# Six of 36 input loads issued as two transfers (rows 0 to 119 and rows 120 to 127) in a retention and token-mixing kernel

## The chip, the cores and the metric

The kernel runs on one core of a Trainium2 chip. The metric is the device time of one execution in microseconds (us), as the median of several runs. TensorE is called PE below, VectorE DVE, ScalarE ACT, GpSimd POOL; SyncE (SP) issues the transfers (DMAs) between HBM and on-chip memory.

## What is computed

Two stages. The first is a retention recurrence over the tokens of each of 4 batches and 8 heads, with 64 x 64 states:

```python
for t in range(S):                      # S = 768
    state = gamma * state + outer(k[t], v[t])
    y[t] = scale * q[t] @ state
```

The second stage takes x, the heads of y side by side (4 x 768 x 512), and mixes tokens:

```python
W_tok = scale * (x @ w_q) * (x @ w_k)   # einsum bsd,btd->bst
out = relu(W_tok @ x) @ w_out
```

q, k and v are float32 of shape 4 x 8 x 768 x 64 each, the output is float32 of shape 4 x 768 x 512.

## The kernel before

The 768 tokens of a batch are cut into three **pairs** of two chunks of 128 tokens, 12 pairs in all (0 to 11). Each pair needs a load of q, of k and of v, so there are 36 loads of 512 KB. A pair has a kind (`KINDS`): R, 2 or M. A load (function `load`) fills one slot of the tile `stage`, 128 partitions x 1024 floats. In q and k loads of every kind, and in v loads of kinds R and 2, one transfer brings the whole slot: partition g gets tokens 2g and 2g+1 of all eight heads, so 8 pieces of 512 bytes for each of 128 partitions. A v load of kind M (pairs 9, 10 and 11) takes four transfers of 128 KB. The first v load is split over two issuing engines, ACT and SP; SP issues every other transfer, in one queue.

Everything runs in an order written out by hand (`ORDER`): each word of it is a step, and each engine takes its own steps in that order. `Lk.4=11` is the load of k of pair 4 into slot 11. SP's order is v0, k0, q0, q1, k1, k2, q2, v1, q3, k3, v2, k4, v3, W (the two small weights), q4, q5, k5, v4, LO (w_out, in four pieces), v5, k6, q6, q7, v6, k7, v7, k9, q8, k8, q9, v8, v9, k11, q10, k10, v10, q11, v11, and then 15 stores of the output. The loads up to v7 go into fresh slots; from k9 on a load first waits until its slot has been read, and a store until its slot has been written.

A load is followed by casts to bf16: `ck` and `cq` make `ks` and `qs` of k and q (line 145 on ACT, 146 on DVE and POOL), `cv` makes `vs` of v with the decay factors `fv` (lines 380 and 399, mostly on POOL). On PE follow the transposes of k and q (lines 471 to 517), the scores `sc` (line 556), the state update `st` (line 590, from `ks` and `vs`), the two halves of y (`in` lines 629 to 650, `ia` lines 669 and 683), and the second stage: transposes of x (713, 719), `wqk` (746, 757), `zm` (783), `mx` (802), and the output projection `pj` (824), whose results go back into `stage` for the stores (line 216). `fill` (line 345) are matmuls on a tile of zeros that stand at fixed places of the order. DMA lines are 188 (whole loads), 183 (v of kind M), 198 and 205 (weights), 216 (stores).

Of the kernel before, what the change touches and what calls it, by code (L numbers as in the profile page):

```python
# [63 lines left out]
SLOTS = 27  # L64
U = 2
PAD = 224
BUFS = dict(
    ks=6, vs=6, qs=4, kT=3, qT=3, at0=2, at1=2, s=4, x=6, xT=3, m=7, z=2, relu=4,
)
# [5 lines left out]
def kernel(  # L75
# [21 lines left out]
    B, H, S, D = q.shape  # L97
# [14 lines left out]
    def pool(name, bufs, **kw):  # L112
        return ctx.enter_context(tc.tile_pool(name=name, bufs=bufs, **kw))


    pool("pad", 1).tile([128, PAD], FP32, name="pad")
    stage_pool = pool("stage", 1)
    const_pool = pool("const", 1)
    pools = {name: pool(name, bufs) for name, bufs in BUFS.items()}
    psum = pool("psum", 1, space=bass.MemoryType.PSUM)  # L120
# [27 lines left out]
    def rows(i):  # L148
        return slice(i * 64, i * 64 + 64)
# [6 lines left out]
    def tokens(p):  # L156
        b, cp = divmod(p, NP)
        return b, slice(cp * 2 * C, (cp + 1) * 2 * C)

    def load(name, p, slot, part=None, eng=None):  # L160
        eng = eng or nc.sync
        b, ts = tokens(p)
        src = {"k": k, "q": q, "v": v}[name][b, :, ts, :]
        st = stage[:, slot]
        pairs[p][name + "_st"] = st
        cs = range(2) if part is None else (part,)
        hs = slice(0, H) if part is None else slice(part, H, 2)
        if name == "q" and U == 8:
            f = slice(0, 2) if part is None else part
            eng.dma_start(  # L170
                out=st.rearrange("p (x f) -> p x f", x=2)[:, f],
                in_=src.rearrange("h (t u) d -> t h (u d)", u=U)[:, hs],
            )
        elif KINDS[p] == "N" and name != "q":
            for c in cs:
                eng.dma_start(
                    out=st[:, 512 * c : 512 * c + 512].rearrange("t (h d) -> t h d", d=D),
                    in_=src[:, C * c : C * c + C].rearrange("h t d -> t h d"),
                )
        elif KINDS[p] == "M" and name == "v":  # L180
            for c in cs:
                for j in range(2):
                    eng.dma_start(
                        out=st[rows(j), 512 * c : 512 * c + 512].rearrange("g (h d) -> g h d", d=D),
                        in_=src[:, C * c : C * c + C].rearrange("h (g j) d -> j g h d", j=2)[j],
                    )
        else:
            eng.dma_start(  # L188
                out=st.rearrange("g (h f) -> g h f", h=H)[:, hs],
                in_=src.rearrange("h (g j) d -> g h (j d)", j=2)[:, hs],  # L190
            )

    wstages = {}

# [15 lines left out]
    def store(p, c=None):  # L210
# [5 lines left out]
        nc.sync.dma_start(out=dst, in_=src, max_dma_last_dim=OBYTES)  # L216

    load(*FIRST, 0, nc.scalar)
    load(*FIRST, 1, nc.sync)


# [76 lines left out]
    if U > 2:  # L298
# [3 lines left out]
            out=ident_q.rearrange("p (c hp t) -> p c t hp", c=2, hp=HP),  # L302
            in_=identity.rearrange("p (c t hp) -> p c t hp", c=2, hp=HP),
# [16 lines left out]
    for cp in range(NP):  # L320
        nc.vector.tensor_copy(
            out=fy1.rearrange("p (cp x) c hp -> p cp x c hp", x=2)[:, cp].rearrange("p x c hp -> p c x hp"),
            in_=fy[:, 2 * cp : 2 * cp + 2].rearrange("p c (hp x) -> p c x hp", x=2),
# [521 lines left out]
    for token in ORDER:  # L845
        token, _, slot = token.partition("=")
        token, _, b = token.partition("@")
        token, _, e = token.partition(":")
        name, *args = token.split(".")
        if b:  # L850
            b = ["ab".index(i) if i in "ab" else int(i) for i in b]
        args = [int(i) for i in args]
        if name == "fill":
            fill(args[0], b[0])
        elif name == "W":
            W(e)
        elif name in ("Lk", "Lq", "Lv"):
            load(name[1], args[0], int(slot))
        elif name == "LW":
            load_w(int(slot))  # L860
        elif name == "LO":
            load_wo(args[0], int(slot))
        elif name == "S":
            store(*args)
        elif name == "eo":
            eo(e, b, *args, slot=int(slot))
        else:
            steps[name](e, b, *args)
# [30 lines left out]
```

## Time and profile before

| | |
|---|---|
| median of 3 runs | 101.84 us (101.64 to 101.92) |
| profiled execution | 101.69 us, of which 99.8 us from the first to the last instruction (the span) |
| PE busy | 89.9 us, 90% of the span |
| DVE, ACT, POOL busy | 74.2, 70.1, 51.8 us |
| moved by DMA | 26.73 MB in 47169 packets, mean 268 GB/s |
| read from HBM, written | 20.19 MB, 6.29 MB |
| granted PE clock | 1.0 throughout |

A row of the profile gives the line of the code, the engine, the operation and its tiles (out<-in). A name with a q behind an engine (SPq) is that engine's sequencer, here SP issuing a transfer. The time that a row of SPq shows is the time that the issue took on SP, not the time until the data lands.

### The profile page before, as it was taken

The page shows a single profiled execution, that of the slowest core. Times are in us where ns is not written, and L with a number is a line of the kernel's source. Part 1 is how long each engine was busy: PE and PEld are TensorE (multiplying, and loading weights), DVE is VectorE, ACT ScalarE, POOL GpSimd, SP SyncE. Part 2 cuts the span into 40 slices and gives each one's busy share as a digit, 9 for nine tenths or more (in the row PEclk, how much of TensorE's full clock was granted, in tenths as well). Part 3 has the DMA queues.
Part 4 walks back from the last instruction along what each step waited for, and adds up shares of the span by engine and source line. Part 5 has one row for each costly group of instructions (what it writes and reads, how often), then busy time and mean ns, then how long its engine had stood idle before and what let it go on. Part 6 is the DMA issues. An engine that isn't in the chain of part 4 may idle for free.

```text
span 99.8 us, 3840 instructions
## 1 busy us (share of the span) xinstructions
PE 89.9 (90%) x1642; PEld 59.9 (60%) x1642; DVE 74.2 (74%) x123; ACT 70.1 (70%) x124; POOL 51.8 (52%) x68
## 2 busy tenths in 40 slices
PE   5996999999599979989998997999999999999940
PEld 1335476587488656676786473676786775754310
DVE  6495789998677998897669887889869865360340
ACT  5245694599769799956588967899669785339720
POOL 6091318253892968958499999977892000000000
PEclk9999999999999999999999999999999999999999
DMA  0999999999999999999998999989933920591793
GB/s 19 301 346 348 346 347 344 323 275 267 277 319 340 335 314 268 321 269 248 335 257 242 322 215 343 314 219 249 343 140 146 406 91 0 212 393 35 305 396 140
DMA packets 47169, 26.73 MB, mean 268 GB/s; under 512 B 8240, under 2 KB 44080, under 8 KB 47152
## 3 DMA queue, kind: packets, MB, share of 16 engines
q1 hardware_dynamic: 46624, 26.22, 86.7%
q10 hardware_dynamic: 528, 0.26, 0.9%
q8 instruction: 13, 0.21, 0.8%
q14 instruction: 4, 0.03, 0.1%
HBM read 20.19 MB, written 6.29 MB: 265 GB/s over the span
## 4 chain that ended last, share of the span: by engine, by line
SPq 40%; PE 36%; DMA 8%; POOL 4%; ACT 3%; DVE 3%; issue 2%; DVEq 0%; POOLq 0%
SPq L188 35%; PE banks L824 17%; DMA stage<-in_v_dram 8%; POOL vs L399 4%; SPq L205 3%; PE banks L746 2%; PE banks L757 2%; SPq L198 2%; PE banks L556 2%; DVE relu L819 2%; PE banks L683 2%; PE banks L802 2%; ACT relu L817 2%; PE banks L590 2%; PE banks L719 1%
## 5 line engine op out<-in xcount | busy, mean ns | idle before, releaser
L399 POOL TENSOR_TENSOR vs<-stage,fv 64x512 bf16<-64x512 f32 x22 | 23.7, 1075 | 9.3 <-DMA stage<-in_v_dram 8.2
L574 DVE TENSOR_TENSOR at<-banks,maskR 128x1024 bf16<-128x1024 f32 x18 | 21.7, 1219 | 3.5 <-PE banks L556 3.5
L824 PE MATMUL banks<-wout_sb,relu 128*128 128x512 bf16 x96 | 23.7, 381 | 0.3 <-DVE relu L819 0.2
L145 ACT CAST ks<-stage 64x512 bf16<-64x512 f32 (+1 forms) x25 | 15.5, 619 | 4.5 <-DMA stage<-in_k_dram 4.1
L704 DVE TENSOR_TENSOR x<-banks,fy 128x1024 bf16<-128x1024 f32 x12 | 14.6, 1220 | 1.0 <-PE banks L683 0.6
L145 ACT COPY stage<-banks 128x512 f32<-128x512 f32 x19 | 11.0, 587 | 5.8 <-PE banks L824 5.7
L824 PEld LDWEIGHTS <-relu 128*128 128x128 bf16 x96 | 8.3, 99 | 9.3 <-issue 0.8
L345 PE MATMUL banks<-warm 128*128 128x512 bf16 x38 | 11.7, 444 | 1.4 <-DVE warm L224 1.2
L817 ACT ACTIVATE relu<-banks 128x512 bf16<-128x512 f32 x18 | 10.0, 603 | 3.6 <-PE banks L802 2.2
L146 POOL CAST ks<-stage 64x512 bf16<-64x512 f32 (+1 forms) x15 | 9.1, 609 | 5.2 <-DMA stage<-in_k_dram 4.6
L145 ACT CAST qs<-stage 128x512 bf16<-128x512 f32 x14 | 8.4, 619 | 2.9 <-DMA stage<-in_q_dram 2.7
L380 POOL TENSOR_TENSOR vs<-stage,fv 128x512 bf16<-128x512 f32 x6 | 6.2, 1047 | 5.8 <-DMA stage<-in_v_dram 5.8
L590 PE MATMUL banks<-vs,ks 128*64 128x64 bf16 (+1 forms) x200 | 6.9, 198 | 1.8 <-POOL vs L399 1.6
L574 DVE TENSOR_TENSOR at<-banks,mask 128x1024 bf16<-128x1024 f32 x6 | 7.1, 1218 | 1.0 <-ACT ks L145 0.8
L146 DVE COPY qT<-banks 128x1024 bf16<-128x1024 bf16 x8 | 5.5, 687 | 2.9 <-PE banks L517 1.9
L590 PEld LDWEIGHTS <-ks 128*64 128x64 bf16 (+1 forms) x200 | 4.9, 110 | 4.4 <-issue 3.0
L345 PEld LDWEIGHTS <-warm 128*128 128x128 bf16 x38 | 3.9, 111 | 5.9 <-issue 3.0
L757 PE MATMUL banks<-wqk_w,xT 128*128 128x64 bf16 x96 | 7.3, 244 | 0.0
L145 ACT CAST s<-banks 128x256 bf16<-128x256 f32 x16 | 6.0, 377 | 1.8 <-PE banks L590 1.8
L145 ACT COPY kT<-banks 128x1024 bf16<-128x1024 bf16 x6 | 6.1, 1012 | 1.8 <-PE banks L471 1.7
L746 PE MATMUL banks<-xT,wqk_w 128*128 128x256 bf16 x48 | 7.3, 274 | 0.0
L556 PE MATMUL banks<-qT,kT 64*128 64x128 bf16 x144 | 6.7, 217 | 0.6 <-ACT kT L145 0.5
(79 smaller groups left out, 152.5 us busy)
## 6 DMA issues: line engine op xcount, KB each, us to landing
stage<-in_k_dram SPq DMA_DIRECT2D x12, 512.0 KB, 6.8
stage<-in_q_dram SPq DMA_DIRECT2D x12, 512.0 KB, 6.1
out_dram<-stage SPq DMA_DIRECT2D x9, 512.0 KB, 3.9
stage<-in_v_dram SPq DMA_DIRECT2D x8, 512.0 KB, 6.6
stage<-in_v_dram SPq DMA_DIRECT2D x12, 128.0 KB, 4.6
out_dram<-stage SPq DMA_DIRECT2D x6, 256.0 KB, 2.2
stage<-in_moe_w_out_dram SPq DMA_DIRECT2D x4, 256.0 KB, 5.3
stage<-in_v_dram ACTq DMA_DIRECT2D x1, 256.0 KB, 4.0
```

What stands on the lines that cost most here:

```text
L145: return nc.scalar.copy(out=out, in_=in_)
L146: return ENGINES[e].tensor_copy(out=out, in_=in_)
L188: eng.dma_start(out=st.rearrange("g (h f) -> g h f", h=H)[:, hs], in_=src.rearrange("h (g j) d -> g h (j d)", j=2)[:, hs],)
L345: nc.tensor.matmul(out=bank32(b), lhsT=warm[:, 0:128], rhs=warm, start=True, stop=True)
L399: eng.tensor_tensor(out=st["vs"][rows(j), c].rearrange("p hp x d -> p (hp x) d"), in0=src[rows(c), :, j], in1=fv[rows(c), cp, :, j].to_bro ...
L574: ENGINES[e].tensor_tensor(out=st["at", half].rearrange("p x hi j t -> p x (hi j t)").rearrange("p x (n f) -> p x n f", n=n), in0=st["at_p ...
L590: nc.tensor.matmul(out=state_ps[rows(x), hp, :], lhsT=st["ks"][rows(c), hp, j, x, :] if two else st["ks"][:, c, hp, x, :], rhs=st["vs"][ro ...
L704: ENGINES[e].tensor_tensor(out=dst, in0=src, in1=f.to_broadcast([128, 2, H, D]), op=ALU.mult)
L746: nc.tensor.matmul(out=ps[:, 128:384], lhsT=wqk_sb[:, a, 0 : 2 * DH], rhs=st["xT"][:, a].rearrange("p c t -> p (c t)"), start=(a == 0), st ...
L757: nc.tensor.matmul(out=wk[:, c], lhsT=st["xT"][:, a, c, :], rhs=wqk_sb[:, a, 2 * DH :], start=False, stop=(a == NDM - 1), skip_group_check ...
L817: nc.scalar.activation(out=st["relu", c], in_=src, func=ACT.Relu)
L824: nc.tensor.matmul(out=bank32(b[0]), lhsT=st["relu", c][:, a // 2, a % 2, :], rhs=wout_sb[:, a, :], start=(a == 0), stop=(a == NDM - 1),)
```

## The change

Six loads, the q loads of pairs 1, 5, 6 and 10 and the k loads of pairs 4 and 9, are each issued as two transfers into the same slot: one of partitions 0 to 119 (480 KB) and behind it one of partitions 120 to 127 (32 KB). The bytes, the 512-byte pieces, the slots and the order of the loads are as before. SP issues six transfers more. The instructions of the four other engines are the same as before, in the same order, apart from what they wait for: a reader of a split slot waits for both transfers.

```diff
 PAD = 224
+SPLIT = ('q1', 'k4', 'q5', 'q6', 'k9', 'q10')
+SPLITS = (slice(0, 120), slice(120, 128))
...
         else:
-            eng.dma_start(
-                out=st.rearrange("g (h f) -> g h f", h=H)[:, hs],
-                in_=src.rearrange("h (g j) d -> g h (j d)", j=2)[:, hs],
-            )
+            to = st.rearrange("g (h f) -> g h f", h=H)
+            fr = src.rearrange("h (g j) d -> g h (j d)", j=2)
+            for g in SPLITS if name + str(p) in SPLIT else (slice(0, 128),):
+                eng.dma_start(out=to[g, hs], in_=fr[g, hs])
```

What stands on SP, first at the head of its queue, before the change. The tiles are the slot and the input; the shape is partitions x heads x floats, and x2 stands for two rows that read alike (q0 and q1, then k1 and k2):

```order
L188 DMA stage<-in_v_dram 128x4x128
L188 DMA stage<-in_k_dram 128x8x128
L188 DMA stage<-in_q_dram 128x8x128 x2
L188 DMA stage<-in_k_dram 128x8x128 x2
L188 DMA stage<-in_q_dram 128x8x128
```

The same place after it (the line number is 193 now):

```order
L193 DMA stage<-in_v_dram 128x4x128
L193 DMA stage<-in_k_dram 128x8x128
L193 DMA stage<-in_q_dram 128x8x128
L193 DMA stage<-in_q_dram 120x8x128
L193 DMA stage<-in_q_dram 8x8x128
L193 DMA stage<-in_k_dram 128x8x128 x2
```

q1 has become two rows; k1, and everything behind it, stands one place later.

Further down the same queue, before: k3, v2, k4, v3, the two small weights, q4 and q5, k5, v4.

```order
L188 DMA stage<-in_k_dram 128x8x128
L188 DMA stage<-in_v_dram 128x8x128
L188 DMA stage<-in_k_dram 128x8x128
L188 DMA stage<-in_v_dram 128x8x128
L198 DMA stage<-in_moe_w_q_dram 128x4x64
L198 DMA stage<-in_moe_w_k_dram 128x4x64
L188 DMA stage<-in_q_dram 128x8x128 x2
L188 DMA stage<-in_k_dram 128x8x128
L188 DMA stage<-in_v_dram 128x8x128
```

And after:

```order
L193 DMA stage<-in_k_dram 128x8x128
L193 DMA stage<-in_v_dram 128x8x128
L193 DMA stage<-in_k_dram 120x8x128
L193 DMA stage<-in_k_dram 8x8x128
L193 DMA stage<-in_v_dram 128x8x128
L200 DMA stage<-in_moe_w_q_dram 128x4x64
L200 DMA stage<-in_moe_w_k_dram 128x4x64
L193 DMA stage<-in_q_dram 128x8x128
L193 DMA stage<-in_q_dram 120x8x128
L193 DMA stage<-in_q_dram 8x8x128
L193 DMA stage<-in_k_dram 128x8x128
L193 DMA stage<-in_v_dram 128x8x128
```

k4 and q5 have become two rows each. From v3 on every transfer has two more ahead of it than before, from k5 on three.

## The prediction

> **What bounds the kernel now.** I read the page first, then the chain that ended last, then SP's rows in order of time, and last what PE and POOL wait for. From the page, the span, PE's share and the chain by engine:
>
> ```profile
> span 99.8 us, 3840 instructions
> PE 89.9 (90%) x1642; PEld 59.9 (60%) x1642; DVE 74.2 (74%) x123; ACT 70.1 (70%) x124; POOL 51.8 (52%) x68
> SPq 40%; PE 36%; DMA 8%; POOL 4%; ACT 3%; DVE 3%; issue 2%; DVEq 0%; POOLq 0%
> ```
>
> PE is busy 90% of the span, yet the chain goes through SP's issues for 40% of it. The two fit together when the chain is read in order of time (start, length, what):
>
> ```profile
> 0.73 0.44 SPq L188
> ...
> 1.23 0.49 SPq L188
> ...
> 39.20 3.00 SPq L188
> ...
> 42.25 7.59 DMA stage<-in_v_dram
> ...
> 54.38 0.32 PE banks L590 x8
> ```
>
> Up to the v load issued at 42.25 (v7) the chain is one issue of SP after another; v7 lands at 42.25 + 7.59 = 49.84, and from 54.38 on the chain stays almost wholly on PE. So loads set the pace of the first half, PE that of the second, and a load that lands earlier is worth what PE stands idle for it. SP's own rows (start, length, line, operation, tiles, count) show how the loads are paced:
>
> ```profile
> 13.95 1.45 SPq L188 DMA_DIRECT2D stage<-in_v_dram  x1
> 15.44 2.54 SPq L188 DMA_DIRECT2D stage<-in_k_dram  x1
> 18.02 1.40 SPq L188 DMA_DIRECT2D stage<-in_v_dram  x1
> ...
> 25.56 2.29 SPq L188 DMA_DIRECT2D stage<-in_v_dram  x1
> ...
> 32.28 2.28 SPq L188 DMA_DIRECT2D stage<-in_k_dram  x1
> ...
> 39.20 3.00 SPq L188 DMA_DIRECT2D stage<-in_k_dram  x1
> 42.25 1.41 SPq L188 DMA_DIRECT2D stage<-in_v_dram  x1
> ...
> 46.72 3.01 SPq L188 DMA_DIRECT2D stage<-in_k_dram  x1
> ```
>
> An issue of 512 KB with empty queues took 0.49 (the chain's k0 at 1.23); in the full stream it takes 1.45, so SP is held back by the queues for about a microsecond of each. Five loads are held longer: k4 2.54, v4 2.29, k6 2.28, k7 3.00, k8 3.01. Against 1.45 that is 1.09, 0.84, 0.83, 1.55 and 1.56 us, the first four of them, 4.31 us, ahead of v7. What else is moved at those times? The queue for instructions, on the whole page and then in the windows from 16 to 17.3, 25.9 to 27 and 32.5 to 33.6 us (packets, MB, share of 16 engines); the window from 40.3 to 41.4 gives the last row again:
>
> ```profile
> q8 instruction: 13, 0.21, 0.8%
> q8 instruction: 1, 0.02, 4.5%
> q8 instruction: 1, 0.02, 5.2%
> q8 instruction: 1, 0.02, 5.5%
> ```
>
> In each of these windows one packet of program text is fetched, as one of the 13; 4.5% of 16 engines' time in 1.3 us is 0.94 us of one engine, 5.5% in 1.1 us is 0.97. What it does to the data, by stretches (us, busy times by engine, clock, DMA share, GB/s):
>
> ```profile
> 14.00:16.20 2.20, 2.20 (x62) 1.53 (x59) 2.06 (x4) 1.14 (x2) 0.78 (x1) 1.00 1.15 347
> 21.00:23.00 2.00, 2.00 (x46) 1.74 (x38) 2.00 (x3) 1.94 (x4) 2.00 (x2) 1.00 0.94 261
> ```
>
> The full stream moves 347 GB/s; some 5 us after k4's long issue there is a dent of a quarter. My reading: one DMA engine is busy with program text for almost a microsecond, its queue of data stays full, SP cannot finish an issue that needs room on every engine, and all other engines run short once they reach that place of the stream.
>
> **What the change does, part by part.** *The 120 rows.* If a load gives each of 16 engines 8 of its 128 rows, 120 rows fill 15 engines and one gets none; the 8 rows behind it can go to other engines, one row each. Per split one engine has then 8 rows less to do, 1.45 us at the stream's pace, and up to eight engines one row more, 1.45 / 8 = 0.18 us. If the engine that was spared is the one that is behind, it catches up by a whole load, and SP isn't held for it. [...]
>
> *Which stalls are in reach.* A split helps against a stall while it is among the transfers in flight. A load lands up to 7.59 us after its issue starts (v7, above), so it reaches a stall that is at most that late: k4 its own stall (1.09), q5, issued just ahead of v4, that one (0.84), q6, issued at about 34.6, that of k7 at 39.20 (1.55). k6's 0.83 comes before q6 is issued; q1 has no stall behind it. So up to 1.09 + 0.84 + 1.55 = 3.48 us go ahead of v7, and four splits add 4 x 0.18 = 0.72: v7 lands up to 2.76 earlier. v3 (issued at 18.02) has q1 and k4 ahead: 1.09 - 0.36 = 0.73 earlier. q7, which follows q6, has 1.09 + 0.84 - 0.72 = 1.21.
>
> *What PE gets of it.* PE's idle times in this stretch, in order of time (idle time and who ended it in brackets), and POOL's before them:
>
> ```profile
> 26.78 0.32 PE L590 MATMUL banks<-vs,ks 128*64 128x64 bf16 x8 [1.16 <-POOL vs L399]
> 36.16 0.32 PE L590 MATMUL banks<-vs,ks 128*64 128x64 bf16 x8 [0.21 <-ACT s L145]
> 37.08 0.39 PE L802 MATMUL banks<-m,z 64*128 64x256 bf16 x4 [0.37 <-ACT kT L145]
> 45.04 0.41 PE L517 MATMUL banks<-identity,qs 64*128 64x64 bf16 x16 [0.48 <-POOL qs L146]
> 54.38 0.32 PE L590 MATMUL banks<-vs,ks 128*64 128x64 bf16 x8 [0.47 <-POOL vs L399]
> 24.57 2.16 POOL L399 TENSOR_TENSOR vs<-stage,fv 64x512 bf16<-64x512 f32 x2 [1.52 <-DMA stage<-in_v_dram]
> 43.81 1.17 POOL L146 CAST qs<-stage 128x512 bf16<-128x512 f32 x2 [1.11 <-DMA stage<-in_q_dram]
> 49.98 4.35 POOL L399 TENSOR_TENSOR vs<-stage,fv 64x512 bf16<-64x512 f32 x4 [1.31 <-DMA stage<-in_v_dram]
> ```
>
> PE waits 1.16, 0.48 and 0.47 us for POOL, which each time has just waited for a load (v3, q7, v7). Earlier landings take 0.73 of the first, all 0.48 of the second (1.21 is more) and all 0.47 of the third (2.76 is more): 1.68 us. The two waits for ACT, 0.21 + 0.37 = 0.58, are not DMA's; they stay. The cover is thin: at 26.78 only POOL's 2.16 us stand between landing and PE, and when a load comes sooner ACT or DVE, busy 70 and 74%, are late next. So I take two thirds, 1.1 us, with 0.73 (the first wait alone) and 2.26 (1.68 + 0.58) as ends.
>
> *The six issues.* Nearest rows are the 0.44 of the first 256 KB and 0.49 of k0, so 0.44 each is an upper price for 32 KB; below is 0. Five of them fall where SP is held by the queues for 1.45 - 0.49 = 0.96 us per load, which hides them; if that cover went, they would cost 5 x 0.44 = 2.2 us. q10's stands where SP waits for slots:
>
> ```profile
> 57.70 0.81 SPq L188 DMA_DIRECT2D stage<-in_q_dram  x1
> 58.60 1.64 SPq L188 DMA_DIRECT2D stage<-in_k_dram  x1
> ```
>
> Behind it k10 is held by the queues again (1.64), so I count nothing. Behind every added issue only SP's own queue waits. The readers of a split slot wait for a second landing, behind the first by one row's time, 0.18, which is in the sum already.
>
> The sum: the profiled execution took 101.69 us, span 99.8 and 1.89 around it. 101.69 - 1.1 = 100.6; the median of the runs, 101.84, lies 0.15 above that execution, so the forecast is **100.7 us**.
>
> **The rivals.** *The spared engine is not the late one* (slower). Then no stall goes, and each split only adds its row to engines that share the pace: v3 lands 0.36 later, q7 and v7 0.72 later. All three end waits of PE, so PE is up to 0.72 later at 54.38 and keeps that to the end; k9 and q10 add up to 0.36 more for the last loads. It decides as soon as the late engine is any of those that still get eight rows: 101.84 + 0.6 = 102.4, at most 101.84 + 1.08 = 102.9. For it speaks that no view names the engine, and that the program text fetched between 21 and 23 us leaves the issues around it (v3's 1.40) short, as if a different engine had been hit. Against it: the stalls of 1.55 and 1.56 are longer than the 0.97 of a fetch. An engine that had kept pace would have to lose its lead first, and would hold SP for less than its own halt; a longer hold fits an engine that was behind already, so one that is hit repeatedly. [...]
>
> *Nothing changes.* All engines share one stream, the 8 rows take what the 120 leave, and PE's other waits fill the gaps: 101.84 plus or minus 0.3. [...] Against it: the dent of 261 against 347 GB/s shows engines without work, so the stream isn't full and has room to gain.
>
> **How the numbers follow.** The forecast's case, that a late engine is relieved, gets 0.50: the long stalls speak for a lasting straggler, and a split takes eight rows off one engine for one row on others. The wrong engine gets 0.33, nothing 0.17. About 0.3% (0.31 us) is what a measurement of this kernel can tell from no change. Nearly all of the first case is faster, nearly all of the second slower, and the third is mostly the same: faster 0.50, same 0.14, slower 0.36. The first case alone spans 101.84 - 2.26 = 99.6 to 101.84 - 0.36 = 101.5. Over all cases the range is 99.6 to 102.6, which leaves out the upper end of the wrong-engine case and a gain beyond all of PE's five waits.
>
> **What would show it.** Right: k4's two issues together near 1.45 + 0.4 instead of 2.54, no issue of 3.00 at k7, v3 and v7 landing earlier, PE's wait of 1.16 at 26.78 down to about 0.4. Wrong engine: the same long issues after each fetch, v7 landing about 0.7 later, and a PE wait above 1.16. Wrong altogether if v7 lands much earlier and the end doesn't move: then PE's second half has a wait of its own that the early half only covers.

## The result, and the profile after

The changed kernel takes 105.38 us, median of 4 runs (104.96 to 105.93); the kernel before took 101.88 (101.64 to 102.22, 4 runs beside them). The ratio is 1.0344, interval 1.0279 to 1.041: slower by about 3.5 us, and above the range that was given. The profiled execution took 105.93 us, its span 104.2. Here and in the experiments a ratio can differ from that of the two medians, since it leaves out executions that were disturbed and the medians do not.

From the page of the changed kernel: span, engines, packets, and the chain by engine:

```profile
span 104.2 us, 3834 instructions
PE 90.3 (87%) x1626; PEld 60.4 (58%) x1642; DVE 74.4 (71%) x123; ACT 70.0 (67%) x124; POOL 51.8 (50%) x68
DMA packets 47211, 26.73 MB, mean 257 GB/s; under 512 B 8282, under 2 KB 44122, under 8 KB 47194
SPq 41%; PE 22%; DMA 15%; ACT 7%; POOL 6%; issue 4%; DVE 1%; ACTq 0%; POOLq 0%; DVEq 0%
```

PE does about the same work (90.3 us, 89.9 before) and stands idle for 104.2 - 90.3 = 13.9 us of the span instead of 99.8 - 89.9 = 9.9. So the computing itself took 0.4 us more, and PE waits 4.0 us more. Of the chain, PE has 22% where it had 36%, and waits for transfers have 15% instead of 8%.

The number of packets bears on how the pieces were spread. The page before counts 47169, 42 fewer with the same bytes; all 42 are below 512 B:

```profile
DMA packets 47169, 26.73 MB, mean 268 GB/s; under 512 B 8240, under 2 KB 44080, under 8 KB 47152
```

If every transfer ends with one small packet per engine, a load over 16 engines has 16 of them, and one that is cut has 15 + 8 = 23: six times 7 more is 42. That fits the prediction's count of engines. In the changed kernel the stretch from 6.75 to 7.75 us holds 16 packets below 512 B and that from 8.50 to 10.25 us 23, by the order of the queue those of q0 and of q1. The kernel that cuts the six loads by heads (below) fits as well: its page counts 47265 packets, 96 more than before, which is six times 16.

Now the pace of the stream, in stretches of the changed kernel (us; busy time of PE, PEld, DVE, ACT, POOL; clock; DMA share; GB/s), and behind it one stretch of before. The DMA share is the time of all packets as a share of the time of 16 engines; in the full stream it is above 1:

```profile
5.00:7.00 2.00, 2.00 (x7) 0.80 (x6) 1.99 (x2) 0.53 (x1) 1.76 (x2) 1.00 1.15 347
8.00:10.00 2.00, 1.19 (x23) 1.05 (x24) 1.16 (x3) 0.62 (x1) 0.03 (x1) 1.00 1.22 219
...
21.00:23.20 2.20, 2.19 (x72) 2.00 (x72) 2.20 (x3) 2.15 (x4) 0.39 (x1) 1.00 1.13 217
```

```profile
8.00:10.00 2.00, 1.41 (x24) 1.16 (x25) 0.96 (x4) 1.11 (x3) 0.00 (x0) 1.00 1.15 347
```

While the 120 rows of q1 and of k4 are moved, the rate falls from 347 to 219 and 217 GB/s, and the DMA engines are as busy as ever (share 1.22 and 1.13, against 1.15). So they do not lack work: the packets themselves take longer. That is the new thing in this profile. Before, the first of these stretches ran at 347; from 21 to 23 us there was the prediction's dent (261), but with a share of 0.94, so with engines short of work. In the first of the two stretches 2.0 x (347 - 219) = 256 KB less were moved, worth 0.74 us at 347; in the second 2.2 x (347 - 217) = 286 KB, 0.82 us, of which the dent of before already had 2.0 x (347 - 261) = 172 KB, 0.50 us.

SP's rows of the changed kernel (start, length, line, operation, tiles, count):

```profile
1.77 4.62 SPq L193 DMA_DIRECT2D stage<-in_q_dram  x3
6.44 1.74 SPq L193 DMA_DIRECT2D stage<-in_k_dram  x2
8.23 2.33 SPq L193 DMA_DIRECT2D stage<-in_q_dram  x1
...
16.79 3.42 SPq L193 DMA_DIRECT2D stage<-in_k_dram  x2
...
27.59 2.15 SPq L193 DMA_DIRECT2D stage<-in_v_dram  x1
...
41.66 2.58 SPq L193 DMA_DIRECT2D stage<-in_k_dram  x1
44.28 1.88 SPq L193 DMA_DIRECT2D stage<-in_v_dram  x1
```

The issues that were held at a fetch of program text are still held: k4's two together 3.42 (one load before: 2.54), v4 2.15 (2.29), k7 2.58 (3.00), though each now has a cut load in flight around it. New is 2.33 for q2, an uncut load that is issued while q1's 120 rows are being moved; before, its issue took 1.45. v7 is issued at 44.28 instead of 42.25.

What became of it at the end of the chain, and at PE and ACT, in the changed kernel (chain: start, length, what; the others with idle time and releaser in brackets):

```profile
44.28 8.26 DMA stage<-in_v_dram
...
60.91 7.24 DMA stage<-in_q_dram
68.78 1.01 ACT qT L147
```

```profile
13.23 0.61 PE L457 MATMUL banks<-identity,ks 128*128 128x128 bf16 x8 [0.53 <-ACT ks L147]
27.74 0.27 PE L641 MATMUL banks<-s,qT 64*128 64x64 bf16 x4 [1.29 <-ACT s L147]
33.91 0.38 PE L558 MATMUL banks<-qT,kT 64*128 64x128 bf16 x7 [0.73 <-ACT xT L147]
45.72 0.20 PE L519 MATMUL banks<-identity,qs 64*128 64x64 bf16 x1 [0.57 <-ACT qs L147]
...
69.83 0.60 PE L748 MATMUL banks<-xT,wqk_w 128*128 128x256 bf16 x4 [1.40 <-ACT qT L147]
68.25 0.62 ACT L147 CAST qs<-stage 128x512 bf16<-128x512 f32 x1 [1.70 <-DMA stage<-in_q_dram]
```

v7 lands at 44.28 + 8.26 = 52.54, 2.70 later than before (49.84). The second piece of q10 lands at 68.15; ACT has stood idle for it for 1.70 us, PE behind ACT for 1.40. Before, neither had a wait at that place:

```profile
63.75 0.62 ACT L145 CAST qs<-stage 128x512 bf16<-128x512 f32 x1
...
65.57 0.60 PE L746 MATMUL banks<-xT,wqk_w 128*128 128x256 bf16 x4
```

Summed over all of PE's idle stretches of 0.1 us or more, its waits go from 5.85 to 8.71 us; the rest of the 4.0 lies in shorter gaps. The largest growth is that one (1.40), then the waits at 33.91 (0.73) and 13.23 (0.53), for which before has no row.

### The profile page after: what moved, and what is told of

Its sections match the earlier page's. It is cut to its first block, busy times and chain, and to the rows that moved or that the text cites. A ratio compares the mean times of both kernels' runs of the same rounds, so it can differ in the third digit from the quotient of the medians.

```text
span 104.2 us, 3834 instructions
## 1 busy us (share of the span) xinstructions
PE 90.3 (87%) x1626; PEld 60.4 (58%) x1642; DVE 74.4 (71%) x123; ACT 70.0 (67%) x124; POOL 51.8 (50%) x68
## 4 chain that ended last, share of the span: by engine, by line
SPq 41%; PE 22%; DMA 15%; ACT 7%; POOL 6%; issue 4%; DVE 1%; ACTq 0%; POOLq 0%; DVEq 0%
SPq L193 34%; PE banks L826 11%; DMA stage<-in_v_dram 8%; DMA stage<-in_q_dram 7%; SPq L207 5%; POOL vs L401 4%; SPq L200 3%; PE banks L748 2%; ACT relu L819 2%; PE banks L759 2%; DVE relu L821 1%; ACT stage L147 1%; POOL ks L148 1%; ACT qT L147 1%; PE banks L558 1%
## 5 line engine op out<-in xcount | busy, mean ns | idle before, releaser
L826 PE MATMUL banks<-wout_sb,relu 128*128 128x512 bf16 x84 | 22.9, 381 | 0.9 <-DVE relu L821 0.2
L148 POOL CAST qs<-stage 128x512 bf16<-128x512 f32 x9 | 5.4, 611 | 2.9 <-ACT stage L147 1.4
```

The source lines that it names most:

```text
L148: return ENGINES[e].tensor_copy(out=out, in_=in_)
L826: nc.tensor.matmul(out=bank32(b[0]), lhsT=st["relu", c][:, a // 2, a % 2, :], rhs=wout_sb[:, a, :], start=(a == 0), stop=(a == NDM - 1),)
```

## The experiments

The theory after the result: while a piece of 120 rows is moved, the stream itself is slower, and the cause is which rows are written at the same time. The rivals: a second issue or a second landing costs more than thought; fewer than 16 engines, or fewer rows to an engine, are what costs; or the reading of other rows is slow. The six loads are named by input and pair: q1, k4, q5, q6, k9, q10. The line that all the edits touch is the loop over `SPLITS` in the load, and the set `SPLIT` of the loads that it is applied to.

**Loads alone, cut in every way.** Twelve rounds of eight loads of 512 KB, the pieces differing by round:

```
STAGES = [whole,
  [(slice(0, 120), EVERY), (slice(120, 128), EVERY)],
  [(slice(0, 120), EVERY)],
  [(slice(120, 128), EVERY)],
  [(slice(0, 128), slice(0, 7)), (slice(0, 128), slice(7, 8))],
  [(slice(0, 64), EVERY), (slice(64, 128), EVERY)],
...
```

> Only loads, no computation (the output is copied from a stage slot and is not the reference's). Twelve rounds of eight loads, each round waiting for the one before: whole; 120+8 rows; 120 alone; 8 alone; heads 0-6 + head 7; 64+64; 64 alone; 96+32; 112+16; rows 8-127 alone; whole; whole. Theory 'rows' (a piece of 120 rows is dealt to the engines so that they hinder each other): whole 340 to 350 GB/s, 120 rows alone 200 to 250 GB/s with all engines busy, heads 7+1 above 320. Theory 'extra transfer' (a second issue and landing costs, whatever is in it): 120 alone about 340, and 120+8, heads 7+1, 64+64, 96+32, 112+16 all alike, near 512 KB per 2.1 us (250 GB/s).

The rate in the steady part of eight of the rounds (us; DVE, ACT, POOL, all idle; clock; DMA share; GB/s). In order: whole; 120 + 8 rows; 120 rows alone; heads 0 to 6 and head 7 of all rows; 64 + 64; 96 + 32; 112 + 16; rows 8 to 127 alone:

```profile
13.00:18.00 5.00, 0.00 (x0) 0.00 (x0) 0.00 (x0) 1.00 1.15 346
33.00:42.00 9.00, 0.00 (x0) 0.00 (x0) 0.00 (x0) 1.00 1.17 222
52.00:60.00 8.00, 0.00 (x0) 0.00 (x0) 0.00 (x0) 1.00 1.16 221
79.00:86.00 7.00, 0.00 (x0) 0.00 (x0) 0.00 (x0) 1.00 1.14 341
96.00:103.00 7.00, 0.00 (x0) 0.00 (x0) 0.00 (x0) 1.00 1.24 241
130.00:136.00 6.00, 0.00 (x0) 0.00 (x0) 0.00 (x0) 1.00 1.24 270
146.00:153.00 7.00, 0.00 (x0) 0.00 (x0) 0.00 (x0) 1.00 1.22 292
161.00:170.00 9.00, 0.00 (x0) 0.00 (x0) 0.00 (x0) 1.00 1.17 223
```

And SP's last row of the rounds whole, 120 + 8, 8 rows alone, heads, 64 + 64, and 112 + 16:

```profile
17.98 1.45 SPq L224 DMA_DIRECT2D stage<-in_k_dram  x1
...
40.40 2.39 SPq L224 DMA_DIRECT2D stage<-in_k_dram  x2
...
70.53 0.30 SPq L224 DMA_DIRECT2D stage<-in_k_dram  x1
...
84.67 1.45 SPq L224 DMA_DIRECT2D stage<-in_k_dram  x2
...
101.52 2.06 SPq L224 DMA_DIRECT2D stage<-in_k_dram  x2
...
151.75 1.71 SPq L224 DMA_DIRECT2D stage<-in_k_dram  x2
```

A load cut into 120 + 8 rows takes 2.39 us of the stream, a whole one 1.45: 0.94 us per split. With nothing else going on, the 120 rows alone run at 221 GB/s; the 8 rows behind them are not what costs. A load that is cut by heads has two issues and two landings as well and takes 1.45, at 341 GB/s. So the second issue is hidden, as predicted, and the loss is in which rows a transfer holds. Whole loads at the end of the run are back at 347 GB/s. Two equal pieces do not help (64 + 64: 241), nor does it matter which end the eight rows are taken from (8 to 127: 223).

**Loads alone, one range of rows for each round.** Is it the number of rows, or which rows? The edit is the list again:

```
[(slice(a, b), EVERY)] for a, b in ((0, 128), (0, 64), (32, 96), (64, 128), (0, 32), (48, 80),
                                    (0, 96), (32, 128), (0, 112), (16, 128), (0, 60), (0, 128))
```

> Only loads again, twelve rounds of eight, each of one range of partitions alone: 0-127, 0-63, 32-95, 64-127, 0-31, 48-79, 0-95, 32-127, 0-111, 16-127, 0-59, 0-127 (the output is not the reference's). [...]

The same columns; rows 0 to 127, 0 to 63, 32 to 95, 64 to 127:

```profile
14.00:20.00 6.00, 0.00 (x0) 0.00 (x0) 0.00 (x0) 1.00 1.14 344
29.00:36.00 7.00, 0.00 (x0) 0.00 (x0) 0.00 (x0) 1.00 1.23 213
41.00:46.00 5.00, 0.00 (x0) 0.00 (x0) 0.00 (x0) 1.00 0.96 280
52.00:59.00 7.00, 0.00 (x0) 0.00 (x0) 0.00 (x0) 1.00 1.23 212
```

Three ranges of 64 rows each: the first and last move 213 and 212 GB/s with a DMA share of 1.23, the middle one 280 with a share of only 0.96. The author's estimate for rows 32 to 95, if it is the rows that decide, was 320 to 350 GB/s, and it is missed. By the share, 0.96 against 1.14 for the whole load, the engines have some idle time there, so it is not their packets that limit the rate; what does is not shown. 280 / 0.96 = 292 GB/s per unit of share is close to the whole load's 344 / 1.14 = 302, against 213 / 1.23 = 173. Same count of rows and of bytes, other partitions, and the packets run at nearly full speed again. The number of rows cannot do that. What differs is which rows are moved. In every round the partitions that are written and the rows of the input that are read have the same numbers, so the reading is not set aside by a run; against it speaks that the input's rows lie alike in all three.

The other ranges of this run: 276 GB/s for rows 0 to 95, 267 for 32 to 127, 260 for 0 to 111 and 288 for 16 to 127; 217 for 0 to 31, 204 for 48 to 79 and 199 for 0 to 59.

The ranges of 96 and 112 rows move 260 to 288 GB/s, those of 32 and 60 rows 199 to 217. Of the three with 64 rows, 32 to 95 (280) stands with the first, 0 to 63 and 64 to 127 (213 and 212) with the second, so the number of rows alone does not order them. The 120 rows do not fit into this order either: they move 221 GB/s, less than the 260 of 0 to 111, which is part of them. That the rows of a piece set its rate is shown; why 120 rows are nearly as slow as 0 to 63 is not, and no view names the engine of a row.

**The same six loads, cut by heads.** Two issues and two landings as in the change, but all 128 rows in both:

```diff
-            for g in SPLITS if name + str(p) in SPLIT else (slice(0, 128),):
-                eng.dma_start(out=to[g, hs], in_=fr[g, hs])
+            for x in (slice(0, 7), slice(7, 8)) if name + str(p) in SPLIT else (hs,):
+                eng.dma_start(out=to[:, x], in_=fr[:, x])
```

> The same six loads are issued as two transfers, but cut by heads (heads 0 to 6 and head 7, all 128 partitions each) instead of by partitions. Theory 'rows': near the kernel before, 101.6 to 102.6 us. Theory 'extra transfer': as slow as the change, 105 to 106 us.

Measured: 101.68 us, ratio 0.9871 (0.9789 to 0.9953). It isn't slower, which ends the rival of the second issue and landing. Whether it is really faster took a repetition in five rounds:

> The cut by heads once more, with more rounds. If its gain of 1.3% was real: 100.2 to 101.0 us; if it was noise of that chip: within 0.3% of the kernel before.

Measured: 101.89 us, ratio 1.004 (0.9995 to 1.0085). The gain did not come again. In the profiled execution of this kernel the stretch in which q1 is moved runs at full pace:

```profile
8.00:10.00 2.00, 1.49 (x25) 1.23 (x26) 0.96 (x4) 1.06 (x3) 0.00 (x0) 1.00 1.14 344
```

344 GB/s where the change has 219. Cutting six other loads by heads (k1, q2, k5, q7, k8, q9) tells whether it matters which loads are cut:

> Six other loads (k1, q2, k5, q7, k8, q9) cut by heads 7+1. If two transfers instead of one help by themselves: as fast as the cut of the change's six, 100.2 to 101.2 us. If the gain hangs on which loads and where program text is fetched: within 0.5% of before.

Measured: 101.56 us, ratio 1.0038 (0.9957 to 1.012): no difference.

**64 + 64 rows.** Two equal pieces:

```diff
-SPLITS = (slice(0, 120), slice(120, 128))
+SPLITS = (slice(0, 64), slice(64, 128))
```

> The same six loads cut into partitions 0 to 63 and 64 to 127. [...] If only the odd count of 15 engines matters: 101.6 to 102.6 us. Theory 'extra transfer': 105 to 106 us.

Measured: 105.06 us, ratio 1.0237 (1.0102 to 1.0373). Slower here too. In the kernel before, the count comes out at 16 small packets for every transfer, the twelve of 64 partitions among them: its 8240 packets below 512 B are 7168 pieces of 256 bytes (14 transfers of 128 KB) and 67 transfers times 16. If that holds for these pieces and stands for 16 engines, it isn't the one engine left out of 120 rows that decides.

**112 + 16 rows.**

```diff
-SPLITS = (slice(0, 120), slice(120, 128))
+SPLITS = (slice(0, 112), slice(112, 128))
```

> The same six loads cut into partitions 0 to 111 and 112 to 127. In the loads-only kernel such a pair took 1.71 us in steady stream against 1.45 of a whole load, 0.26 more (120+8: 0.94, 64+64: 0.61). Theory 'rows': cost in proportion to these, counted from the cut by heads (1.4 us below before): 6 x 0.26 = 1.6 above it, so 101.3 to 102.8 us. Theory 'any cut by partitions costs the same': 105 us.

Measured: 103.6 us, ratio 1.0185 (1.0127 to 1.0243). The expected range is missed on its upper side. The order is right: 0.26 us per split in the loads alone (1.71 against 1.45) against 0.94, and a ratio between that of the heads and that of 120 rows. The sizes are not in proportion: six times 0.26 is 1.6 us, and 103.6 - 101.8 = 1.8 are lost here, while six times 0.94 is 5.6 and only 3.5 are lost.

**Rows 32 to 95 first.** The same six loads in three pieces, the middle one the range that moved 280 GB/s by itself:

```diff
-SPLITS = (slice(0, 120), slice(120, 128))
+SPLITS = (slice(32, 96), slice(0, 32), slice(96, 128))
```

> The same six loads in three transfers each: partitions 32 to 95, 0 to 31 and 96 to 127. [...] Rival, pieces cost by their number: above 64+64, over 105 us.

Measured: 103.23 us, ratio 1.0169 (1.0105 to 1.0232). The author's estimate was 103 to 104.3 us. More transfers than in any other version and yet less loss than 120 + 8 (1.0344). Of the outer pieces, rows 0 to 31 moved 217 GB/s by themselves. The interval overlaps that of 64 + 64, so this run supports the theory that the rows decide but doesn't carry it; the loads alone do.

**Fewer of the six.** Which of the splits make the loss? The edit is the set, first the four ahead of v7:

```diff
-SPLIT = ('q1', 'k4', 'q5', 'q6', 'k9', 'q10')
+SPLIT = ('q1', 'k4', 'q5', 'q6')
```

> Only q1, k4, q5 and q6 are split at 120; k9 and q10 are whole. If each split costs the stream about the same and PE sees most of it: four sixths of 3.5 us, so 103.8 to 104.6 us. If the end is set by the last two (q10, whose 7.24 us landing stands in the chain): near 102 to 103 us.

Measured: 104.53 us, ratio 1.0274 (1.0189 to 1.036). The rest was then tried in the same way: q1 alone, the last two, q10 alone, and all but q10.

> Only q1 is split at 120. It costs the stream 0.94 us once, near the start. If everything behind it moves as one: 0.7 to 0.9 us above the kernel before. If PE's later work and its fills cover it: within 0.3 us of before.

Measured: 103.92 us, ratio 1.019 (1.0114 to 1.0266).

> Only k9 and q10 are split at 120. From the change (3.4%) less the first four (2.7%): 0.5 to 1.0 us above before. If what is late at the end is q10's second piece, whose landing stands in the chain of the changed kernel: 1.0 to 1.5 us. If the second half is PE's alone: within 0.3 us.

Measured: 104.34 us, ratio 1.0311 (1.0247 to 1.0375).

> Only q10 is split at 120. In the kernel with k9 and q10 split PE waits 2.01 us at 68.95 for the transpose of q10, where it did not wait before. If q10 alone does that: 1.5 to 2.2 us above the kernel before. If it takes the lateness of k9 in front of it: 0.5 to 1.0 us.

Measured: 103.37 us, ratio 1.0264 (1.0187 to 1.0341).

> All but q10 are split at 120. First four: 2.7% slower; k9 comes later in the stream. If the delays of early and late splits overlap (PE, already late, finds q10 landed): 2.7 to 3.3% slower, so little less than all six. If q10 adds its own 2 us to whatever came before: 1.3 to 2% slower.

Measured: 105.08 us, ratio 1.0383 (1.0282 to 1.0484).

The first four came out in the range that was expected if each split costs about the same. The others did not: q1 alone, the last two and the five each cost more than was expected of them, q10 alone more by its ratio, though not by the medians (103.37 - 101.61 = 1.8 us). And the parts do not add up: four cost 2.7%, two 3.1%, six 3.4%. The last two, by the profile of their kernel, act at two places. One is q10's landing (ACT, then PE, with idle time and releaser in brackets):

```profile
67.37 0.62 ACT L147 CAST qs<-stage 128x512 bf16<-128x512 f32 x1 [2.31 <-DMA stage<-in_q_dram]
68.95 0.60 PE L748 MATMUL banks<-xT,wqk_w 128*128 128x256 bf16 x4 [2.01 <-ACT qT L147]
```

The other is v7, which is whole and issued just ahead of k9 (its entry in the chain, and PE's wait for what POOL makes of it):

```profile
42.68 8.25 DMA stage<-in_v_dram
...
55.47 0.32 PE L592 MATMUL banks<-vs,ks 128*64 128x64 bf16 x8 [1.12 <-POOL vs L401]
```

PE waited 0.47 us there before, and v7 took 7.59 us from issue to landing. In the three kernels with k9 cut into 120 + 8 it takes 8.25 (the last two), 8.26 (all six) and 8.61 (all but q10), each from one execution. So in these a split cost the load just ahead of it as well, and the working counted only loads behind it.

With q10 alone cut, its landing costs less (the same two rows as first above):

```profile
65.22 0.62 ACT L147 CAST qs<-stage 128x512 bf16<-128x512 f32 x1 [0.72 <-DMA stage<-in_q_dram]
66.80 0.60 PE L748 MATMUL banks<-xT,wqk_w 128*128 128x256 bf16 x4 [0.43 <-ACT qT L147]
```

PE waits 2.01 us here when only the last two loads are cut, 1.40 with all six, 0.43 with q10 alone. A PE that comes late anyway waits less for q10: it gets here at 68.43 with all six cut (69.83 - 1.40), at 66.94 with the last two. That fits the overlap of the two halves of the change. It does not explain all: with q10 left whole the time is no better (1.0383 against 1.0344, intervals overlapping), and q10's own wait of 0.43 is less than the 1.8 us or 2.6% that its split costs. Part of such a difference is one execution against another: the profiled execution with q10 alone cut starts this step 1.23 us later than that of before (66.80 against 65.57), but it starts the state update behind v7 0.56 us late already (54.94 against 54.38), when q10 has not been issued (57.90). How 0.94 us of one load become 1.8 us or more of the whole stays open. It may be that a shift of one engine against the other four meets PE's fixed order of work at many places by a little; the runs don't tell.

## Where the prediction was right and wrong

**The count of engines fits, and the path was right.** 15 engines for 120 rows and 8 for 8: the 42 small packets more agree with it, though no view names an engine. Loads do set the pace of the first half, and PE's idle time is where it shows (13.9 us against 9.9).

**The six issues, at nothing: right.** A load cut by heads takes 1.45 us like a whole one, and six such cuts give 1.004 (0.9995 to 1.0085).

**The step that failed is the first, "the 120 rows".** It priced a split at "up to eight engines one row more, 1.45 / 8 = 0.18 us", and it took for granted that 15 engines move 8 rows each as fast as they do in a whole load. No run shows the 0.18; the runs showed 0.94 us in its place, five times as much. The rows' places in the memory were no part of the working, and its 347 GB/s hold for transfers of all 128 partitions; the loads of before that the working read are all of that kind, and nothing bounded the price of another shape. (The twelve transfers of 64 partitions that before has, on line 183, were not read; they move in pieces of 256 bytes and need not have given the price of this one.) The bound from above was therefore not a bound. Four splits ahead of v7 come to 3.76 us at 0.94, not 0.72. v7 landed 2.70 later: its issue came 2.03 later, and it took 0.67 longer from issue to landing, with k9's 120 rows behind it.

**The relief of 3.48 us did not come.** After the change v4, k7 and k8 are still held, and a fetch lies in the same place. The queue for instructions from 27.5 to 29, 42.4 to 44 and 49.4 to 50.8 us of the changed kernel (packets, MB, share of 16 engines):

```profile
q8 instruction: 1, 0.02, 3.9%
q8 instruction: 1, 0.02, 4.7%
q8 instruction: 1, 0.02, 4.3%
```

The windows hold v4 (2.15), k7 (2.58) and k8:

```profile
49.76 2.23 SPq L193 DMA_DIRECT2D stage<-in_k_dram  x1
```

k7 and k8 are held 0.42 and 0.78 us less than before (3.00 and 3.01), far from the 1.45 that a relieved engine would have given by the author's estimate; it can be as well that a slower stream has more room. Nor are these holds fixed: in the kernel with q10 alone cut, where every load up to here is whole, v4 is held 3.40, k6 1.14, k7 1.65 and k8 2.00 (before: 2.29, 2.28, 3.00, 3.01). The 3.48 us were summed from one execution. Which engine a fetch occupies, and whether it is always the same, stays open: no view names it. So the condition of the rival that forecast a slower kernel, that the spared engine isn't the late one, is neither shown nor excluded, and its price, 102.4 to 102.9, fell short for the same reason as the forecast's: both took 0.18 per split.

**"PE's second half" was wrong in one place.** The last splits were counted at nothing, or at 0.36 in the rival; q10's landing became the last load on the chain, and PE waits 1.40 us for it. Before, that load had a cover that the prediction didn't size: it landed 5.6 us after its issue, at 63.3, and its first reader started at 63.75, so the cover was about 0.4 us, less than the 0.94 of one split.

**The range** has a slip of its own, which decides nothing here: the low end of the forecast case's gain is 0.73 us in the sum and 0.36 in the range.

**"Nothing changes"** took it that the 8 rows take what the 120 leave. The measured price of a pair is above nothing: 0.61 us per 512 KB for 64 + 64 (2.06 against 1.45), 0.94 for 120 + 8.

## What to carry to other kernels

If a load of all 128 partitions has to be cut, try the cut along the free dimension first: here it kept the full rate (341 against 346 GB/s), while a cut by partitions cost 0.26 us (112 + 16), 0.61 (64 + 64) and 0.94 (120 + 8) per 512 KB. Before moving a shape that no row of the profile shows, measure its rate by itself in a kernel of loads alone; the one that was run here gives the price of eight shapes at once. And where the DMA share is as high as ever but the GB/s are down (here 1.22 at 219, against 1.15 at 347), look first at which partitions are moved at the same time, and only then at queues and issues. Look at the loads just ahead of a slow one too (here v7: 8.25 to 8.61 us against 7.59), not only at those behind it.

## What the runs showed of the hardware

- Transfers of 120 partitions in packets of 512 B moved 221 GB/s, transfers of 128 moved 346, with the same share of busy DMA time (1.16 and 1.15): it is as if each packet took more than half as long again (346 / 221 = 1.57).
- Of 64 partitions, 32 to 95 ran at nearly the whole load's rate per share of busy time (292 against 302 GB/s), 0 to 63 and 64 to 127 at less than six tenths of it (173 and 172).
- An 8-row piece took SP 0.30 us to issue in a round of such pieces alone (the row at 70.53), and a second issue and landing of the same load (the cut by heads) cost nothing that these runs could measure (1.45 us for both issues and for one, ratio 1.004).
- A transfer in its slow shape slowed the loads around it too: q2, a whole load, was held for 2.33 us while q1's 120 rows were in flight (1.45 before), and v7, issued ahead of k9's 120 rows, landed 8.25 to 8.61 us after its issue (7.59 before).
